# A fused routing-attention and two-layer kernel: three weight conversions moved to the second block, transposed rows through another PSUM bank, the last product in two column halves

## The chip, the cores and the metric

The kernel runs on one core of a Trainium2 chip. The metric is device time in microseconds. The kernel before takes 992.72 us, the median of three runs (991.85 to 994.62). The profiled execution has a span of 994.2 us, and all positions below are counted from the start of that span.

## What is computed

Four batches of eight heads attend over 768 tokens of 64 numbers each. Every query and key is assigned to the nearest of 16 centroids of its head, and a query sees only the keys of its own centroid. The heads, side by side, form rows of 512 numbers that go through two dense layers with a leaky activation. Cut to its core:

```python
q_assign = argmax(einsum('bhsd,hcd->bhsc', q_n, c_n), -1)     # k_assign likewise
mask = q_assign[..., :, None] == k_assign[..., None, :]
attn = softmax(where(mask, q @ k.T / 8, -1e9)) @ v            # (4, 8, 768, 64)
x = attn.transpose(0, 2, 1, 3).reshape(3072, 512)
h = x @ w_in                                                  # 512 -> 2048
g = maximum(h, 0) + alpha * minimum(h, 0)
out = g @ w_out                                               # 2048 -> 512
```

The weights arrive as 64-bit floating-point words. The kernel converts them to FP32 itself.

## The kernel before

**Steps and blocks.** Heads are taken in pairs, four pairs to a batch. For the first three batches the queries are split into two halves of 384, and the unit of work is a step: two key chunks of 128 for one head pair and one half of the queries. Three steps make a pair, twelve steps (`UB`) a block. The first block is half 0 of batch 0, the second is half 1. The last batch is done with the tokens sorted by cluster, so that only neighbouring chunks meet; its pairs are called near here.

A step computes scores into PSUM (`score`, L757, and for the first batch the mask as a product, L766), exponentials on ScalarE (L778), and multiplies the exponentials of the step before with the values (`weigh`, L893; in the first block also the denominators, L886). At the end of a pair `normalise` (L993) writes the transposed attention output xT. While the attention of one block runs, the dense layers of the block before are fed between its pieces: `hidden` (L1017, copied out by L1023, activated by `slopes`, L1009) and `final` (L1035, result copied by L1041 or added by L1043, and stored by L1046). During the first block there is nothing to feed.

**Order.** The order on each engine is written out by hand: the program's text is executed as a list of small pieces, and every engine runs its share in that order. `tick` counts slots, five to a step, and `later(n, piece)` puts a piece n slots further on.

**Conversions.** There are 32, each of 512 columns. `convert` loads raw words (L247, a ring of five raw tiles) and works in three stages: `split` on VectorE (L253 and L255), `scale` on ScalarE (L259 and L261) four slots later, and `join` on VectorE (L265 and L268) followed by a multiply on GpSimd (L271) two slots after that. The intermediate tile `power` comes from a ring of three. The tuple `converting` says how many conversions each of the first block's steps begins; afterwards it is two a step until all are begun. A dense piece that needs a weight which isn't ready runs the missing stages on the spot (`convert_up_to`).

**Cluster masks of the first batch.** `prep_sims` (L381) and `prep_argmax` (L402 to L423) find the clusters of the next pair on VectorE. `of_heads` then issues the copies of the mask to aq (L474, on ScalarE's queue) and computes `outside` (L429, ScalarE). Both are operands of L766 in the next pair's first step.

**PSUM.** The scores have two two-bank tiles (sps), the values' product one bank (vps). Two banks, fps, are shared in turn by `hidden`, `final`, some scores and, before the change, the row transposes. One bank, mps, is handed out by `misc()` and serves the cluster products (L381, L442), the row sums (`total`, L848) and one half of the near product (L926).

**Rows of the near pairs.** For the sorted batch the result goes back to token order. `normalise_near` (L932) writes outT, `to_rows` transposes it twice per pair on TensorE (L955), ScalarE copies it to rows (L958) one slot later, and `put_back` (L963) scatters the rows to memory, from which they are fetched again.

**The end.** The last two blocks' dense layers have no attention beside them. Each does its last eight products per output tile, adds the earlier partial sum and stores 128 rows.

Of the kernel before, what the change touches and what calls it, by code (L numbers as in the profile page):

```python
# [10 lines left out]
FP32 = mybir.dt.float32  # L11
# [5 lines left out]
ALU = mybir.AluOpType  # L17
AX = mybir.AxisListType
PS = bass.MemoryType.PSUM
P = 128  # L20
# [3 lines left out]
def kernel(  # L24
# [11 lines left out]
    nc = tc.nc  # L36

    B, H, S, D = q.shape
    NC = centroids.shape[1]
    DM, DF = moe_w_in.shape  # L40
    NJ = S // P
    NCH = DM // P
    NF = DF // P
    HJ = NJ // 2
# [12 lines left out]
    w_out_sb = wpool.tile([P, NF, DM], FP32, name="w_out_sb")  # L57
# [9 lines left out]
    accp = fast.enter_context(tc.tile_pool(name="accp", bufs=2))  # L67
# [7 lines left out]
    ps_f = fast.enter_context(tc.tile_pool(name="ps_f", bufs=2, space=PS))  # L75
# [8 lines left out]
    def misc():  # L84
        if early:
            early.append(early.pop(0))
            if early[0] is not None:
                return early[0]
        return ps_m.tile([P, 512], FP32, name="mps")
# [5 lines left out]
    def later(slots, piece):  # L95
        due.setdefault(now[0] + slots, []).append(piece)

    def tick():
        now[0] += 1
        for piece in due.pop(now[0], []):  # L100
            piece()
# [7 lines left out]
    Q = 32  # L109
# [52 lines left out]
    for g in range(P // Q):  # L162
        r = slice(g * Q, (g + 1) * Q)
        nc.gpsimd.tensor_copy(
            out=fold[r, :].rearrange("p (a i) -> p a i", i=Q),
            in_=ident[r, None, r].broadcast_to((Q, P // Q, Q)))
# [11 lines left out]
    for h in range(2):  # L178
        nc.vector.tensor_reduce(
            out=pick[:, h:h + 1],  # L180
            in_=fold.rearrange("p (a h c) -> p a h c", h=2, c=NC)[:, 0, h, :],
# [95 lines left out]
    FQ = CW // P  # L277
# [34 lines left out]
    def convert_up_to(n):  # L312
        while converted[0] < n:
            if not under_way:
                convert_next()
            else:
                advance(under_way[0])
# [54 lines left out]
    NX = GT * NG  # L372
# [41 lines left out]
    def prep_argmax(n, ps):  # L414
        top, first, pieces = argmax(ps, exact=n < NCH)
        for piece in pieces:
            piece()
        firsts[n] = first
        if n >= NCH:
            return  # L420
        member = memp.tile([P, HS], BF16, name="member")
        outside = memp.tile([P, 2, HS], BF16, name="outside")
        nc.vector.transpose(out=member, in_=top.rearrange("p t c -> p (t c)"))  # L423

        def of_heads():
            if n > 0:
                prep_queries(n, 0, 0)
            for h in range(2):
                nc.scalar.activation(  # L429
                    out=outside[HP:P, h, :], in_=member[HP:P, :], func=AF.Identity,  # L430
                    scale=pick[HP:P, h:h + 1], bias=pick[HP:P, h + 2:h + 3])

        members[n] = member, outside
        later(12 if n == 0 else 7, of_heads)

    def prep_clusters(n):

# [293 lines left out]
    UB = NCH * SB  # L731
# [50 lines left out]
    def last(m):  # L782

        return waiting[len(waiting) - m:]
# [165 lines left out]

    def to_rows(outT, rows, i):

        ps = ps_f.tile([P, 512], FP32, name="fps")
        for j in range(HJ):
            nc.tensor.transpose(out=ps[:, j * P:(j + 1) * P],  # L955
                                in_=outT[:, (i * HJ + j) * P:(i * HJ + j + 1) * P],
                                identity=ident)
        later(1, lambda: nc.scalar.copy(  # L958
            rows[:, i * HJ:(i + 1) * HJ].rearrange("p j d -> p (j d)"), ps[:, 0:HS]))
# [40 lines left out]
    def ffn_pieces(b, half):  # L1000
        rows = out[b * S:(b + 1) * S, :].rearrange(
            "(p j) n -> p j n" if b == 0 else "(j p) n -> p j n", p=P)
        gs, pss, ys, fresh = {}, {}, {}, deque()


        def slopes():
            while fresh:
                f = fresh.popleft()
                nc.vector.scalar_tensor_tensor(  # L1009
                    out=gs[f], in0=gs[f], scalar=alpha[:, f:f + 1], in1=gs[f],  # L1010
                    op0=ALU.mult, op1=ALU.max)

        def hidden(f):
            convert_up_to((f // FQ + 1) * (NCH + FQ) - FQ)
            ps = ps_f.tile([P, 512], FP32, name="fps")
            for c in range(NCH):
                nc.tensor.matmul(out=ps[:, 0:HS],  # L1017
                                 lhsT=w_in_sb[:, c, f * P:(f + 1) * P],
                                 rhs=xTs[b, half][:, c, :],
                                 start=(c == 0), stop=(c == NCH - 1))  # L1020
            slopes()
            gs[f] = gpool.tile([P, HS], FP32, name="gT")
            nc.scalar.copy(gs[f], ps[:, 0:HS])  # L1023
            fresh.append(f)
            if f % FQ == FQ - 1:
                slopes()

        def final(i, f0, on, off):
            convert_up_to((f0 // FQ + 1) * (NCH + FQ))
            if on:  # L1030
                pss[i] = ps_f.tile([P, 512], FP32, name="fps")
            unfinished[0] = not off
            ps = pss[i]
            for f in range(f0, f0 + FQ):
                nc.tensor.matmul(out=ps[:, 0:DM], lhsT=gs[f][:, i * P:(i + 1) * P],  # L1035
                                 rhs=w_out_sb[:, f, :], start=on and f == f0,
                                 stop=off and f == f0 + FQ - 1)
            if off:
                if i not in ys:
                    ys[i] = ypool.tile([P, DM], FP32, name="y")  # L1040
                    nc.scalar.copy(ys[i], ps[:, 0:DM])  # L1041
                else:
                    nc.vector.tensor_tensor(out=ys[i], in0=ys[i], in1=ps[:, 0:DM],  # L1043
                                            op=ALU.add)
                if f0 + FQ == NF:
                    nc.sync.dma_start(out=rows[:, half * HJ + i, :], in_=ys[i])  # L1046

        hs = [lambda f=f: hidden(f) for f in range(NF)]


        FP = FQ if (b, half) == (0, 0) else NF // 2
        pieces = []
        for f0 in range(0, NF, FP):
            pieces += hs[f0:f0 + FP]
            pieces += [lambda i=i, f=f, f0=f0: final(i, f, f == f0, f + FQ == f0 + FP)
                       for i in range(HJ) for f in range(f0, f0 + FP, FQ)]
        return pieces


# [62 lines left out]
    def feed(pieces):  # L1122
        for _ in range(pieces):
            ffn.popleft()()
# [15 lines left out]
    for u in range(-AHEAD, TOGETHER):  # L1140
        for piece in load_at.get(u, []):
            piece()
        n, half, s = steps[max(u, 0)]
        prior = steps[max(u - 1, 0)]
        ended = u > 0 and prior[2] == SB - 1
        tick()
        if u >= 0:


            score(n, half, range(s, NJ, SB))  # L1150
        tick()
        if ended:
            invert(*prior[:2])
        if u > 0:
            weigh(GROUP, denominators=u <= UB)
        if u >= 0:
            for chunk in last(GROUP):
                mask(chunk)
        if ended:
            normalise(*prior[:2])  # L1160
        if u >= UB:
            if s == 0:
                add_up(last(1)[0], last(2)[0])
            else:
                for chunk in last(GROUP):
                    add_up(chunk)
            if s == SB - 1:
                turn(n, half)
                rows_sums(n, half)
        if u == UB:  # L1170
            early.clear()
            feed_block(u)
            whole = len(ffn) - KEEP
        take = (max(len(ffn) - KEEP - whole * (UB - 1 - u % UB) // UB, 0) if ffn else 0)

        converting = 0 if u < 0 else (2, 0, 2, 2, 0, 2, 2, 1, 1, 1, 2, 2)[u] if u < UB else 2
        for i in range(SLOTS - FIRST):
            tick()
            feed(take * (i + 1) // 3 - take * i // 3)
            if (u, i) == (1 - AHEAD, 0):  # L1180
                cT, alpha = prepare_constants()
            prepare(u, FIRST + i)
            if i < converting:
                convert_next()
            if u >= -1:
                fetch(3 if u < UB else 2)
        if s == SB - 1 and u >= UB:
            total(n)
# [3 lines left out]
    for u in range(TOGETHER, NS + 1):  # L1192
        for piece in load_at.get(u, []):
            piece()
        if u < NS:
            n, half, s = steps[u]
# [49 lines left out]
        for i in slots:  # L1246
# [5 lines left out]
            pieces = len(ffn) - kept(u // UB) + -whole * left // (UB // SB * FREE)  # L1252
# [28 lines left out]
    ps = misc()  # L1281
    for i, p0 in enumerate((0, 1, P // 2, P // 2 + 1)):
        nc.tensor.matmul(out=ps[0:m, i * NN:(i + 1) * NN], lhsT=ident[:, p0:p0 + m],
                         rhs=sorts["begins"], start=True, stop=True)
# [4 lines left out]
                            in1=ident[0:m, m - 1:m], op=ALU.add)  # L1289
# [4 lines left out]
    for i in (1, 3):  # L1294
# [13 lines left out]
                            op=ALU.subtract)  # L1308
    nc.vector.tensor_tensor(out=ends[:, 1, :], in0=ends[:, 1, :], in1=spans[:, 2, :],
                            op=ALU.subtract)  # L1310
# [9 lines left out]
                     start=True, stop=True)  # L1320
# [161 lines left out]
```

## Time and profile before

| what | value |
|---|---|
| time, median of three | 992.72 us |
| span of the profiled execution | 994.2 us |
| TensorE busy | 968.9 us, 97% |
| VectorE busy | 632.0 us, 64% |
| ScalarE busy | 259.2 us, 26% |
| GpSimd busy | 216.8 us, 22% |
| first dense piece L1017, in total | 1024 instructions, 345.4 us |
| second dense piece L1035, in total | 768 instructions, 339.2 us |
| L271, GpSimd multiply of a w_in conversion | 16 instructions, mean 1706 ns |

How to read it: the busy time of TensorE counts matrix instructions from start to a modelled end, so an engine that is busy need not be at its peak rate; one FP32 product is two instructions here, hence twice the counts of the program. The profile also names, for each idle stretch of an engine, the instruction that ended it, and it follows one chain of waits back from the last instruction. A stage's cost is best read from these two together with the busy time of each engine in that stage.

### The profile page before, as it was taken

How to read it: one execution, taken by the hardware profiler on the slowest of the kernel's cores; microseconds unless marked ns; L12 is line 12 of the kernel's file. 1: busy time of each engine (PE TensorE's matmuls, PEld its weight loads, DVE VectorE, ACT ScalarE, POOL GpSimd, SP SyncE). 2: the span in 40 equal slices, each digit the busy share in tenths (PEclk: the TensorE clock that was granted, in tenths of full speed). 3: DMA queues.
4: the chain of work that ended last, by engine and by line, in shares of the span. 5: the costliest groups of instructions: out<-in, count | busy, mean ns of one | idle time of the engine just before them, and what ended most of it. 6: DMA issues, size and time to landing. Idle time of an engine off the chain costs nothing.

```text
span 994.2 us, 10869 instructions
## 1 busy us (share of the span) xinstructions
PE 968.9 (97%) x3947; PEld 480.7 (48%) x3947; DVE 632.0 (64%) x1143; ACT 259.2 (26%) x468; POOL 216.8 (22%) x249
## 2 busy tenths in 40 slices
PE   8988999999999999999999999999999999999997
PEld 5434444445454454545445454454544545455453
DVE  5796788598587776877857698577987532021010
ACT  5665443222121221312222022231232101110110
POOL 2433222010000634401000263630045440000000
PEclk9999999999999999999999999999999999999999
DMA  8434555041200361416020121710621110000000
GB/s 286 145 113 127 130 133 80 17 88 24 33 1 26 97 103 54 85 41 105 1 33 0 53 80 35 136 48 12 90 58 34 33 51 11 0 11 22 0 1 34
DMA packets 174285, 60.45 MB, mean 61 GB/s; under 512 B 161216, under 2 KB 164752, under 8 KB 174224
## 3 DMA queue, kind: packets, MB, share of 16 engines
q1 hardware_dynamic: 168768, 51.42, 24.0%
q0 software_dynamic: 4608, 7.87, 2.4%
q8 instruction: 33, 0.54, 0.2%
q10 hardware_dynamic: 848, 0.39, 0.2%
q14 instruction: 28, 0.23, 0.1%
HBM read 45.15 MB, written 14.16 MB: 60 GB/s over the span
## 4 chain that ended last, share of the span: by engine, by line
PE 90%; DVE 6%; ACT 1%; issue 1%; POOL 1%; ACTq 0%; DVEq 0%; POOLq 0%
PE fps L1017 33%; PE fps L1035 33%; PE vps L893 8%; PE sps L757 8%; PE fps L757 3%; PE mps L381 1%; PE vps L926 1%; PE mps L926 1%; PE sps L766 1%; DVE power L265 1%; ACT gT L1023 0%; DVE w_in_sb L268 0%; PE mps L848 0%; PE fps L354 0%; DVE power L253 0%
## 5 line engine op out<-in xcount | busy, mean ns | idle before, releaser
L1017 PE MATMUL fps<-xT,w_in_sb 128*128 128x384 f32 x1024 | 345.4, 492 | 5.7 <-DVE xT L993 3.0
L1035 PE MATMUL fps<-w_out_sb,gT 128*128 128x512 f32 x768 | 339.2, 596 | 2.2 <-DVE gT L1009 1.1
L1017 PEld LDWEIGHTS fps<-xT,w_in_sb 128*128 128x128 f32 x1024 | 191.4, 191 | 147.0 <-issue 10.0
L1035 PEld LDWEIGHTS fps<-w_out_sb,gT 128*128 128x128 f32 x768 | 143.4, 190 | 173.5 <-issue 161.7
L663 POOL DMA_INDIRECT scratch<-stage,off x96 | 101.4, 1056 | 324.5 <-DMA stage<-in_v_dram 265.9
L1009 DVE SCALAR_TENSOR_TENSOR gT<-gT,alpha 128x384 f32<-128x384 f32 x128 | 80.7, 636 | 140.6 <-ACT gT L1023 134.7
L1023 ACT COPY gT<-fps 128x384 f32<-128x384 f32 x128 | 61.2, 478 | 341.9 <-PE fps L1017 323.5
L757 PE MATMUL sps<-qkT 64*128 64x384 f32 (+1 forms) x512 | 97.9, 499 | 3.1 <-ACT E L778 2.4
L798 DVE SCALAR_TENSOR_TENSOR more<-aq,key,more 128x384 f32<-128x384 bf16 (+1 forms) x136 | 74.4, 605 | 28.8 <-ACT more L778 14.3
L778 ACT ACTIVATE E<-sps 128x768 f32<-128x768 f32 (+1 forms) x81 | 61.2, 803 | 72.6 <-PE sps L766 39.4
L963 POOL DMA_INDIRECT back<-rows,place x48 | 48.4, 1008 | 102.8 <-ACT rows L958 89.4
L757 PEld LDWEIGHTS sps<-qkT 64*128 64x128 f32 x512 | 46.2, 187 | 48.9 <-issue 19.7
L798 DVE SCALAR_TENSOR_TENSOR E<-aq,key,E 128x384 f32<-128x384 bf16 (+1 forms) x104 | 56.6, 600 | 16.8 <-ACT E L778 6.6
L893 PE MATMUL vps<-E,vt 128*64 128x384 f32 x356 | 65.7, 494 | 0.7 <-DVE xT L993 0.7
L1043 DVE TENSOR_TENSOR y<-y,fps 128x512 f32<-128x512 f32 x30 | 20.6, 685 | 69.5 <-PE fps L1035 69.5
L808 DVE TENSOR_TENSOR acc<-acc,E 128x768 f32<-128x768 f32 x47 | 44.9, 955 | 18.3 <-ACT E L778 17.0
L1041 ACT COPY y<-fps 128x512 f32<-128x512 f32 x24 | 14.1, 586 | 138.6 <-PE fps L1035 119.0
L778 ACT ACTIVATE more<-sps 128x768 f32<-128x768 f32 (+1 forms) x47 | 35.5, 797 | 41.8 <-PE fps L1035 21.6
L271 POOL TENSOR_TENSOR w_in_sb<-w_in_sb,power 128x512 f32<-128x512 f32 x16 | 27.3, 1706 | 72.6 <-DVE w_in_sb L268 72.6
L893 PEld LDWEIGHTS vps<-E,vt 128*64 128x64 f32 x356 | 23.0, 136 | 32.6 <-issue 31.0
L893 PE MATMUL vps<-more,vt 128*64 128x384 f32 x220 | 38.8, 491 | 0.0
L757 PE MATMUL fps<-qkT 64*128 64x384 f32 x160 | 35.0, 508 | 0.0
(177 smaller groups left out, 704.3 us busy)
## 6 DMA issues: line engine op xcount, KB each, us to landing
raw<-in_moe_w_in_dram SPq DMA_DIRECT2D x16, 512.0 KB
raw<-in_moe_w_out_dram SPq DMA_DIRECT2D x16, 512.0 KB
out_dram<-y SPq DMA_DIRECT2D x24, 256.0 KB
vt<-in_v_dram SPq DMA_DIRECT2D x12, 384.0 KB
qk<-in_q_dram SPq DMA_DIRECT2D x48, 96.0 KB
qk<-in_k_dram SPq DMA_DIRECT2D x48, 96.0 KB
qk<-scratch SPq DMA_DIRECT2D x32, 96.0 KB
qk<-in_q_dram SPq DMA_DIRECT2D x4, 384.0 KB
```

The lines of the kernel that those rows point to most:

```text
L271: nc.gpsimd.tensor_tensor(out=dst, in0=dst, in1=power[0].bitcast(FP32), op=ALU.mult)
L663: nc.gpsimd.indirect_dma_start(out=scratch[n][1][h * NX + xx], out_offset=bass.IndirectOffsetOnAxis(ap=ranks[n][:, xx, h:h + 1], axis=0), ...
L757: nc.tensor.matmul(out=bank(ps, h, m), lhsT=qkT[r:r + D, S + c * P:S + (c + 1) * P], rhs=qkT[r:r + D, tokens], start=True, stop=not early_ ...
L778: nc.scalar.activation(out=E[:, :, 0:m], in_=ps[:, :, 0:m], func=AF.Exp, scale=SCALE)
L798: nc.vector.scalar_tensor_tensor(out=e, in0=of, scalar=keys[n][:, NJ + c, h:h + 1], in1=e, op0=ALU.is_equal, op1=ALU.mult)
L808: nc.vector.tensor_tensor(out=acc, in0=acc if first is None else first[3], in1=E, op=ALU.add)
L893: nc.tensor.matmul(out=po[r:r + D, 0:HS], lhsT=vts[n][:, h, c, :], rhs=e[:, h, :], start=(c == 0), stop=(c == NJ - 1))
L963: nc.gpsimd.indirect_dma_start(out=to[i], out_offset=bass.IndirectOffsetOnAxis(ap=place[:, h, j:j + 1], axis=0), in_=rows[:, j, h * D:(h + ...
L1009: nc.vector.scalar_tensor_tensor(out=gs[f], in0=gs[f], scalar=alpha[:, f:f + 1], in1=gs[f], op0=ALU.mult, op1=ALU.max)
L1017: nc.tensor.matmul(out=ps[:, 0:HS], lhsT=w_in_sb[:, c, f * P:(f + 1) * P], rhs=xTs[b, half][:, c, :], start=(c == 0), stop=(c == NCH - 1))
L1023: nc.scalar.copy(gs[f], ps[:, 0:HS])
L1035: nc.tensor.matmul(out=ps[:, 0:DM], lhsT=gs[f][:, i * P:(i + 1) * P], rhs=w_out_sb[:, f, :], start=on and f == f0, stop=off and f == f0 + ...
```

## The change

It has three independent parts.

1. Three fewer conversions are begun in the first block, from its seventh step on (14 instead of 17). The second block, which begins two a step until none is left, takes them over. With it `of_heads` comes one slot later for the second to fourth pair, which puts it behind the exponentials of its step in ScalarE's order. The aim is to spread the conversions' work away from the stage where VectorE has most to do.
2. `to_rows` takes its PSUM bank from `misc()` (mps) instead of the ring fps, so that the dense pieces have both banks of fps to themselves.
3. The very last output tile is computed in two halves of 256 columns, each with its own bank, addition and store, the second store on ScalarE's queue. The aim is that the store of the first half runs beside the products of the second, and that the rest after the last product is shorter.

```diff
@@ prep_argmax
-        later(12 if n == 0 else 7, of_heads)
+        later(12 if n == 0 else 8, of_heads)
@@ to_rows
-        ps = ps_f.tile([P, 512], FP32, name="fps")
+        ps = misc()
@@ ffn_pieces
+        def final_columns(i, f0, c0):
+
+            ps = ps_f.tile([P, 512], FP32, name="fps")
+            c = slice(c0, c0 + DM // 2)
+            for f in range(f0, NF):
+                nc.tensor.matmul(out=ps[:, 0:DM // 2], lhsT=gs[f][:, i * P:(i + 1) * P],
+                                 rhs=w_out_sb[:, f, c], start=f == f0, stop=f == NF - 1)
+            y = accp.tile([P, 2 * NX, Q], FP32, name="acc").rearrange(
+                "p x i -> p (x i)")[:, 0:DM // 2]
+            nc.vector.tensor_tensor(out=y, in0=ys[i][:, c], in1=ps[:, 0:DM // 2], op=ALU.add)
+            (nc.scalar if c0 else nc.sync).dma_start(out=rows[:, half * HJ + i, c], in_=y)
...
+        if (b, half) == (B - 1, 1):
+
+            pieces[-(FP // FQ):] = [lambda c0=c0: final_columns(HJ - 1, NF - FP, c0)
+                                    for c0 in (0, DM // 2)]
@@ first block
-        converting = 0 if u < 0 else (2, 0, 2, 2, 0, 2, 2, 1, 1, 1, 2, 2)[u] if u < UB else 2
+        converting = 0 if u < 0 else (2, 0, 2, 2, 0, 2, 1, 1, 1, 1, 1, 1)[u] if u < UB else 2
```

## The prediction, made before the changed kernel was run

> **What bounds the kernel now.** I read the page first: busy shares, then the chain of waits.
>
> ```profile
> PE 968.9 (97%) x3947; PEld 480.7 (48%) x3947; DVE 632.0 (64%) x1143; ACT 259.2 (26%) x468; POOL 216.8 (22%) x249
> ...
> PE 90%; DVE 6%; ACT 1%; issue 1%; POOL 1%; ACTq 0%; DVEq 0%; POOLq 0%
> ```
>
> TensorE (PE) sets the end nearly everywhere; 6% of the chain is VectorE (DVE), some 60 us. The chain in order of time puts most of that before 103 us. So next came busy time by stretch, the end of the first block against the second:
>
> ```profile
> 46.00:60.00 14.00, 13.65 (x124) 5.44 (x120) 13.17 (x28) 8.49 (x14) 3.55 (x4) 1.00 0.28 95
> 60.00:74.00 14.00, 11.26 (x80) 4.43 (x80) 12.56 (x26) 9.31 (x14) 6.25 (x5) 0.88 0.51 156
> 74.00:88.00 14.00, 10.99 (x75) 4.95 (x74) 11.14 (x25) 7.90 (x13) 5.89 (x4) 0.93 0.47 150
> 125.00:150.00 25.00, 25.00 (x96) 11.36 (x93) 21.75 (x36) 12.25 (x20) 7.00 (x5) 1.00 0.62 131
> 150.00:175.00 25.00, 25.00 (x103) 11.81 (x103) 21.66 (x35) 8.44 (x15) 6.60 (x5) 1.00 0.52 74
> 175.00:200.00 25.00, 25.00 (x113) 11.43 (x112) 13.15 (x23) 6.21 (x10) 0.88 (x3) 1.00 0.07 17
> ```
>
> Columns: PE, weight loads, DVE, ScalarE (ACT), GpSimd (POOL), then granted clock. From 46 to 88 us DVE works 37 of 42 us, PE falls to 11 of 14, and its clock to 0.88. From 125 PE is full, and after 175 DVE is half idle. PE's instructions in time order show the price of the first block:
>
> ```profile
> 62.05 2.77 PE L757 MATMUL sps<-qkT 64*128 64x384 f32 x8 [2.40 <-ACT E L778]
> ...
> 86.21 1.62 PE L1017 MATMUL fps<-xT,w_in_sb 128*128 128x384 f32 x2 [3.01 <-DVE xT L993]
> ```
>
> Eight score passes cost 2.77 after an idle 2.40, against 1.56 elsewhere. The chain shows why xT is late: conversions stand in front of it on DVE, and the split L253 waits for POOL's multiply L271.
>
> ```profile
> 79.93 1.29 POOL w_out_sb L271
> 81.22 0.02 issue
> 81.24 0.44 DVE power L253
> ...
> 85.50 0.57 DVE xT L993
> 86.07 0.14 issue
> 86.21 7.71 PE fps L1017 x18
> ```
>
> [...]after the 3.01 us stall 18 passes of L1017 take 7.71 us, 0.428 each, against 0.3225 at full speed (64 in 20.64). [...]a split instruction that runs beside L271 takes 1.49 (45.51 us) instead of 0.42, and that L271 3.45 instead of 1.28. [...]Here the last 256 KB are issued at 988.95, move between 989.5 and 990.6, and the span ends at 994.2.
>
> **Part 1, three conversions out of the first block.** PE's floor there: a step is L757 1.49 + L766 0.43 + L886 0.79 + L893 1.44 = 4.15. From 46.35 (score of step 6): six steps 24.9, L381 0.78, a seventh 4.15, six L1017 passes 1.94 gives 78.1; the pass that waits for xT began at 86.21. That is 8.1 lost, and 7.71 - 18 x 0.3225 = 1.9 by the clock: at most 10.0 to win.
>
> How much does DVE release? Between the normalisations of the second pair (49.19) and of the fourth (83.13) it ran 9 splits and 9 joins; the changed program's order has 6 and 7. A split is 0.67 (51.98 to 52.65), a join 1.20 (to 53.85): 3 x 0.67 + 2 x 1.20 = 4.4. Besides, three waits of L253 for L271 (1.38, 1.18, 1.39) come of the ring of three power buffers: a split needs the multiply of three conversions before. With one conversion a step that multiply is over before the split. Three contended instructions add about 1.1 each. So DVE gives up 4.4 surely, 11.7 at the most.
>
> I followed the new order with these durations. Up to 57.8 (last argmax, L423) nothing moves. The `of_heads` delay of one slot puts step 8's exp (L778, two for 1.51) on ACT ahead of the aq transfers and L429 (1.29), so it starts at 57.4 instead of 61.19 and step 9's score finds its banks free at 59.6: the 2.40 wait goes. What is queued behind: L429 now ends near 60.7, and L766 of step 9, due at 61.1, needs it and aq, which land about 1.2 after their issue ends at 59.4; 0 to 0.4 lost. At steps 2 and 5 the same swap meets PE work that isn't due for over 4 us: nothing. Then the third pair's normalisation ends at 66.1, before L893 needs its bank (66.9), and the fourth's can run 75.2 to 78.1, as L886 ends, against L1017's need at 78.5. DVE has some 3 us of gaps left by then; two contended splits would eat 2 of them and cost PE about 0.9. So 10.0 - 0.4 - 0.9 = **8.7 saved**, bounds 4.4 and 10.0.
>
> What it adds: three conversions in the second block. The rate stays two a step; they only run on to step 20, where DVE has 12 of 25 us free (175 to 200). The order shows none forced by L1017's or L1035's due conversion. Two splits and a join more (2.5 us) ahead of L861/L993 near 176: L993 then waited for PE anyway (0.73), and its bank isn't needed until L893 at 186.35. Joins before a y addition can hold a bank: **0.4 lost**, bounds 0 and 9.5 (three times 1.87 of DVE plus 1.3 of POOL).
>
> **Part 2, rows through mps.** L955 leaves the two-bank ring fps for the single bank mps.
>
> ```profile
> 714.92 2.85 PE L1017 MATMUL fps<-xT,w_in_sb 128*128 128x384 f32 x8 [0.24 <-ACT gT L1023]
> 718.34 0.55 PE L955 MATMUL fps<-ident,qk 128*128 128x128 f32 x3 [0.57 <-ACT gT L1023]
> ...
> 774.34 2.85 PE L1017 MATMUL fps<-xT,w_in_sb 128*128 128x384 f32 x8 [0.68 <-ACT y L1041]
> ```
>
> Removed by the ring: pair 1 0.24 + 0.57 + 0.48 (L1017 at 722.13), pair 2 0.24 + 0.57, pair 3 0.68, pair 4 0.24 + 0.57 + 0.24: together 3.8. Added: the second L955 of a pair waits for the first's copy L958, which stands on ACT behind gT (717.80 and 718.18 there): PE ends at 717.77, L958 at 718.67, so 0.93 with the semaphore. That holds for pairs 1 and 2; in pairs 3 and 4 another piece lies between. In pair 1 L442, on mps too, waits another 0.93 for the second copy. L848 comes a whole piece later: nothing. 3 x 0.93 = 2.8, so **1.0 saved**, bounds -1 and 3.8.
>
> **Part 3, last product by halves.** Eight 512-column products are 16 instructions at 0.4292 (48 in 20.60). By the slope (0.4292 - 0.3225)/128 a 256-column one takes 0.216, and 32 give 6.91 against 6.87. Weight loads (0.19) hide: near 764 L757 sets two 64-row loads per pair of passes at the same rate. Unhidden they would add 6. The first half's addition and transfer lie beside the second half. At the end:
>
> ```profile
> 988.24 0.69 DVE L1043 TENSOR_TENSOR y<-y,fps 128x512 f32<-128x512 f32 x1 [6.18 <-PE fps L1035]
> 988.95 0.33 SPq L1046 DMA_DIRECT2D out_dram<-y  x1
> ```
>
> The addition at 256 columns: L993's 384 take 0.56, so 1 ns a column, 0.43; 0.26 saved. Half the bytes: 0.35 of the 0.7 DMA-busy time. ACT's queue issues in up to 0.60 (L474) against 0.33: 0.1 lost. **0.5 saved**, bounds 0.2 and 0.7.
>
> Sum: -8.7 + 0.4 - 1.0 - 0.5 = -9.8; 992.7 - 9.8 = **983**.
>
> **Rivals.** (a) Everything is won: 10.0 + 2.5 + 0.7, 979.5. For: the order has no ring wait left. Against: mps has one bank. (b) DVE stays the bound and returns only its 4.4: -4.4 + 0.4 - 1.0 - 0.5, 987. For: DVE at 37 of 42 us, and contention that I can't place. (c) The second block gives it back, DVE being at 87% from 125 to 175: +9.5 instead of 0.4, 992.4. Against: PE didn't wait for conversions there. (d) Slower: (b) for the first block, and mps makes every second L955, and the L442 and L848 after them, wait: nine times 0.93 = 8.4 with nothing won from the ring: 992.7 - 4.4 - 0.5 + 8.4 = 996. For: mps serves totals, clusters and the near product as well.
>
> **Chances.** Main 0.62, (a) 0.07, (b) 0.19, (c) 0.07, (d) 0.05. Faster 0.88, same 0.07, slower 0.05. The range takes in (a) and (b) with a measuring spread of about 1, and leaves out (c) and (d): 979 to 988.
>
> **What would show it.** The step-9 score with no wait for L778; no idle before L1017 for xT; that pass near 78.5; granted clock near 1.00 from 60 to 100; L253 not waiting for L271 before 80; L955 waiting 0.9 twice and L442 once; no L1017 waiting for gT from 711 us on (in the old time). It is wrong if DVE stays packed to 80 us with PE waiting, or if PE shows new waits between 100 and 200 us.

## The result, and the profile after

The changed kernel takes **981.87 us**, the median of four runs (981.49 to 982.53), where the kernel before, in runs beside it, takes 992.29 us (991.55 to 994.62). The ratio is 0.9892, with a 95% interval from 0.9874 to 0.991: 10.4 us saved, where 9.8 were forecast. The profiled execution of before was a long one (996.02 us against a median of 992.29), so the two spans, 994.2 and 979.9 us, differ by more than the times do. Some 3 us of the difference are stalls of before's profiled execution; they are told of with the experiment after_again.

The page of the kernel after, busy time and shares of the chain:

```profile
PE 962.9 (98%) x3963; PEld 482.8 (49%) x3963; DVE 635.0 (65%) x1144; ACT 258.7 (26%) x468; POOL 214.9 (22%) x249
...
PE 92%; DVE 5%; issue 1%; ACT 1%; POOL 0%; DVEq 0%; ACTq 0%; POOLq 0%
```

TensorE's share of the chain rises from 90% to 92% and VectorE's falls by a point. The 16 more TensorE instructions are the last product in halves (32 instead of 16). VectorE's busy time even rises by 3 us: the conversions did not go away, they moved. The same stretches as before show where to (span, then PE, weight loads, VectorE, ScalarE, GpSimd, granted clock, DMA share, GB/s):

```profile
46.00:60.00 14.00, 14.00 (x126) 5.74 (x124) 13.50 (x29) 9.63 (x15) 3.75 (x4) 1.00 0.39 115
60.00:74.00 14.00, 12.66 (x112) 5.17 (x110) 12.53 (x26) 9.54 (x15) 8.74 (x5) 1.00 0.57 167
74.00:88.00 14.00, 14.00 (x75) 6.83 (x72) 9.20 (x22) 4.61 (x8) 3.53 (x2) 1.00 0.33 102
150.00:175.00 25.00, 25.00 (x100) 11.71 (x93) 24.40 (x44) 10.63 (x19) 5.41 (x4) 1.00 0.56 87
175.00:200.00 25.00, 24.14 (x111) 10.94 (x112) 19.41 (x33) 7.46 (x13) 3.05 (x4) 1.00 0.08 19
```

From 60 to 88 us PE is now busy 26.66 of 28 us instead of 22.25, at full clock. From 150 to 200 VectorE works 43.81 us instead of 34.81, and PE beside it is busy 49.14 of 50; the 0.86 is one wait of L1035 for gT at 194.27, which before has too, as long, at 202.74. In PE's own order:

```profile
59.44 1.56 PE L757 MATMUL sps<-qkT 64*128 64x384 f32 x8
...
67.71 1.51 PE L893 MATMUL vps<-E,vt 128*64 128x384 f32 x8 [1.34 <-DVE xT L993]
...
77.44 8.01 PE L1017 MATMUL fps<-xT,w_in_sb 128*128 128x384 f32 x24
```

The first line is the score that waited 2.40 for L778; it has no wait left. The third is the dense piece that stood still for 3.01 us in front of its seventh pass; its 24 passes now follow one another. The middle line is what is left: one wait for xT, a pair earlier. Before waits there too, 0.69 at 71.26.

The near stage, where the rows now use the single bank mps:

```profile
708.58 0.55 PE L955 MATMUL mps<-ident,qk 128*128 128x128 f32 x3 [0.95 <-ACT rows L958]
...
712.66 0.25 PE L442 MATMUL mps<-cluster,spread 128*128 128x24 bf16 x4 [0.95 <-ACT rows L958]
...
732.48 0.55 PE L955 MATMUL mps<-ident,qk 128*128 128x128 f32 x3 [0.95 <-ACT rows L958]
...
765.21 0.39 PE L848 MATMUL mps<-parts,fold 128*128 128x48 f32 x2 [0.52 <-ACT gT L1023]
```

Three of these four waits were forecast, at 0.93 each. The waits of L1017 for the ring's gT copy are gone from this stage. And the end of the program:

```profile
967.59 7.07 PE L1053 MATMUL fps<-w_out_sb,gT 128*128 128x256 f32 x32
...
974.69 0.42 DVE L1057 TENSOR_TENSOR acc<-y,fps 128x256 f32<-128x256 f32 x1 [3.03 <-PE fps L1053]
975.15 0.38 ACTq L1058 DMA_DIRECT2D out_dram<-acc  x1
```

The last addition takes 0.42 instead of 0.69, and from its start to the end of the span there are 5.21 us (979.9 less 974.69) instead of 5.96 (994.2 less 988.24).

### The profile page after: what moved, and what is told of

It reads as the page before. It is cut to its first block, busy times and chain, and to the rows that moved or that the text cites. A ratio compares the mean times of both kernels' runs of the same rounds, so it can differ in the third digit from the quotient of the medians.

```text
span 979.9 us, 10900 instructions
## 1 busy us (share of the span) xinstructions
PE 962.9 (98%) x3963; PEld 482.8 (49%) x3963; DVE 635.0 (65%) x1144; ACT 258.7 (26%) x468; POOL 214.9 (22%) x249
## 4 chain that ended last, share of the span: by engine, by line
PE 92%; DVE 5%; issue 1%; ACT 1%; POOL 0%; DVEq 0%; ACTq 0%; POOLq 0%
PE fps L1017 33%; PE fps L1035 33%; PE vps L893 9%; PE sps L757 8%; PE fps L757 3%; PE mps L381 1%; PE vps L926 1%; PE sps L766 1%; PE fps L1053 1%; PE mps L926 1%; DVE power L265 1%; DVE w_out_sb L268 0%; PE vps L201 0%; PE mps L848 0%; PE fps L886 0%
## 5 line engine op out<-in xcount | busy, mean ns | idle before, releaser
L1017 PE MATMUL fps<-xT,w_in_sb 128*128 128x384 f32 x1024 | 342.6, 490 | 0.0
L1035 PE MATMUL fps<-w_out_sb,gT 128*128 128x512 f32 x752 | 332.2, 595 | 1.1 <-DVE gT L1009 1.1
L1017 PEld LDWEIGHTS fps<-xT,w_in_sb 128*128 128x128 f32 x1024 | 190.9, 190 | 138.3 <-ACT more L778 4.4
L1035 PEld LDWEIGHTS fps<-w_out_sb,gT 128*128 128x128 f32 x752 | 140.3, 190 | 168.4 <-issue 158.1
L757 PE MATMUL sps<-qkT 64*128 64x384 f32 (+1 forms) x512 | 96.1, 494 | 0.0
L778 ACT ACTIVATE E<-sps 128x768 f32<-128x768 f32 (+1 forms) x81 | 61.2, 802 | 71.3 <-PE sps L766 39.9
L757 PEld LDWEIGHTS sps<-qkT 64*128 64x128 f32 x512 | 45.7, 186 | 44.5 <-issue 17.4
L893 PE MATMUL vps<-E,vt 128*64 128x384 f32 x356 | 65.7, 494 | 1.3 <-DVE xT L993 1.3
L778 ACT ACTIVATE more<-sps 128x768 f32<-128x768 f32 (+1 forms) x47 | 35.4, 796 | 41.3 <-PE sps L757 40.4
L271 POOL TENSOR_TENSOR w_in_sb<-w_in_sb,power 128x512 f32<-128x512 f32 x16 | 25.4, 1594 | 67.1 <-DVE w_in_sb L268 67.1
L893 PEld LDWEIGHTS vps<-E,vt 128*64 128x64 f32 x356 | 23.0, 136 | 33.3 <-issue 30.7
L893 PE MATMUL vps<-more,vt 128*64 128x384 f32 x220 | 38.8, 491 | 0.0
L271 POOL TENSOR_TENSOR w_out_sb<-w_out_sb,power 128x512 f32<-128x512 f32 x16 | 22.9, 1432 | 57.3 <-DVE w_out_sb L268 57.3
```

The costliest lines, as they stand in the source:

```text
L271: nc.gpsimd.tensor_tensor(out=dst, in0=dst, in1=power[0].bitcast(FP32), op=ALU.mult)
L757: nc.tensor.matmul(out=bank(ps, h, m), lhsT=qkT[r:r + D, S + c * P:S + (c + 1) * P], rhs=qkT[r:r + D, tokens], start=True, stop=not early_ ...
L778: nc.scalar.activation(out=E[:, :, 0:m], in_=ps[:, :, 0:m], func=AF.Exp, scale=SCALE)
L893: nc.tensor.matmul(out=po[r:r + D, 0:HS], lhsT=vts[n][:, h, c, :], rhs=e[:, h, :], start=(c == 0), stop=(c == NJ - 1))
L1017: nc.tensor.matmul(out=ps[:, 0:HS], lhsT=w_in_sb[:, c, f * P:(f + 1) * P], rhs=xTs[b, half][:, c, :], start=(c == 0), stop=(c == NCH - 1))
```

## The experiments

Times of one chip are compared with the kernel before on that chip. There are two questions: does the relief of VectorE before 90 us carry the gain, and why did the near stage win more than its waits add up to? Where two traces are set side by side below, the start of each TensorE instruction in one is compared with the start of the same instruction in the other; this is called the distance between the traces. Each expectation numbers its own theories.

### Each part alone

On a chip where before takes 992.51 us (35 runs). **conv_only** is before with part 1 alone:

```diff
-        later(12 if n == 0 else 7, of_heads)
+        later(12 if n == 0 else 8, of_heads)
...
-        converting = 0 if u < 0 else (2, 0, 2, 2, 0, 2, 2, 1, 1, 1, 2, 2)[u] if u < UB else 2
+        converting = 0 if u < 0 else (2, 0, 2, 2, 0, 2, 1, 1, 1, 1, 1, 1)[u] if u < UB else 2
```

> The kernel before with part 1 alone: the new converting tuple and of_heads one slot later. Theory 1 (the parts add up, and the first block carries most of the gain): 8.5 us less than before, about 983.8, because the two traces stand 8.5 us apart from the first dense pieces on and the second block gives nothing back. Theory 2 (the parts help each other, so that each alone is worth less, and the near pairs carry about half): about 5 us less, 987. A trace of the second block with new PE waits would speak for theory 2.

Measured: 984.19 us, ratio 0.9917 (0.9904 to 0.993), so 8.3 us saved. Part 1 is four fifths of the whole.

**tuple_only** is the second of these two lines without the first.

> The kernel before with the new converting tuple alone; of_heads stays where it was. Theory 1 (VectorE's load is what counts, the exp's place on ScalarE is a smaller term): L429 still stands ahead of step 8's exp, so the score of step 9 waits near 2 us and may lose some clock; 5.5 to 7 us less than before, about 986. Theory 2 (the exp's place is what counts): at most 3 us less, 989 or more.

Measured: 985.16 us, ratio 0.9927 (0.9914 to 0.994), 7.35 us saved, more than expected. PE in its trace:

```profile
61.94 1.62 PE L757 MATMUL sps<-qkT 64*128 64x384 f32 x8 [1.67 <-ACT E L778]
```

Without the slot's delay the score still waits for ScalarE, but 1.67 instead of 2.40, and its eight passes take 1.62 instead of 2.77: the clock was not lost. That leaves about 1 us (8.3 less 7.35) to the delay, and theory 2, the exp's place as the main thing, is out.

**heads_only** is the first of the two lines without the second, on another chip (the second, below), where before takes 996.04 us (22 runs).

> The kernel before with of_heads one slot later and nothing else. Theory 1 (in the kernel before VectorE's queue sets the first block's end, so an earlier exp is absorbed by the wait for xT at L1017): within 0.5 us of before, 992. Theory 2 (the terms add, 7.35 and 8.3 measured with and without it): 1 us less, 991.5. Theory 3 (the wait for the exp and the clock after it are a loss of their own): 3 us less, 989.5.

Measured: 994.86 us, ratio 0.998 (0.9963 to 0.9997), 1.2 us saved, as theory 2 had it. It agrees with what tuple_only lacks against conv_only, though the interval reaches from 0.3 to 3.7 us: as far as these runs can tell, the two edits add up and neither needs the other.

**rows_only** is before with part 2 alone, on the first chip:

```diff
-        ps = ps_f.tile([P, 512], FP32, name="fps")
+        ps = misc()
```

> The kernel before with part 2 alone: to_rows takes the bank of misc(). Theory 1 (the prediction's count, 3.8 us of ring waits removed and 2.8 of waits for the row copy added): 1 us less than before, 991.3. Theory 2 (each stopped dense piece also costs a restart, seen as 2.86 instead of 2.58 for a piece after a wait, so more is removed than was counted): 2 us less, 990.3. Theory 3 (the traces' 4 us over the near pairs is all the bank's doing): 4 us less, 988.3.

Measured: 990.36 us, ratio 0.9978 (0.9971 to 0.9984), 2.15 us saved, twice the 1.0 of the prediction and close to theory 2.

**halves_only** is before with part 3 alone (`final_columns` and the replaced last pieces, as in the diff above).

> The kernel before with part 3 alone: the last output tile in two column halves. Theory 1 (shorter last addition and half the bytes): 0.5 to 0.7 us less than before, 991.7, and 32 passes in 6.9 us. Theory 2 (the second store's issue on ScalarE's queue and its own latency eat it): no change, within 0.2.

Measured: 991.8 us, ratio 0.9994 (0.9985 to 1.0002). The 0.7 us agree with the 0.75 that the traces show at the end, but the interval includes no gain. This kernel still has the ring, and its execution has none of the stalls told of below, so it shows best what an interruption costs:

```profile
712.48 0.49 PE L955 MATMUL fps<-ident,qk 128*128 128x128 f32 x3
713.21 2.85 PE L1017 MATMUL fps<-xT,w_in_sb 128*128 128x384 f32 x8 [0.24 <-ACT gT L1023]
716.63 0.55 PE L955 MATMUL fps<-ident,qk 128*128 128x128 f32 x3 [0.57 <-ACT gT L1023]
```

The number to read is the distance of the starts. From L955 to L1017 it is 0.73 here, and from L1017 to the next L955 3.42. In copy_first_2 (below), which waits for nothing here, the same distances are 0.33 and 2.58 (9.11 less 6.53). So the two interruptions cost 0.40 and 0.84, not 0.24 and 0.57. The page counts idle time from the modelled end of the last matmul, and without a wait the next one begins 0.16 to 0.27 before that end; a wait loses this on top of its bracket. Read so, the nine waits that part 2 removes, 3.8 as shown, were worth about 5.6, and the four that it adds, 3.4 as shown, about 4.1. That makes 1.5 instead of 0.4. Set side by side, the traces show more: from the L1017 at 713.86 to the one at 800.00 (positions of before) rows_only gains 3.96 us on before. Of this, 1.93 is a stall of before between 733 and 737, which halves_only, with the same code there, doesn't have. The remaining 2.03 is part 2, and the 2.15 of the runs agree with it. So an interruption does cost more than its bracket shows, and most of the surplus is this overlap. The changed kernel's first trace gains the same 3.96 on before in this stretch, so half of what the near stage seemed to win there was the stall.

The three parts alone add up to 11.2 us (8.3, 2.15 and 0.7), together they measured 10.4, within what the intervals allow. The traces of before and after, with before's stalls left out, give 8.47, 2.03 and 0.75, again 11.2.

### How many conversions

On the second chip (before 996.04). **dose16** and **dose13a** are the changed kernel with two conversions put back at the end of the first block, and with one more taken out:

```diff
-(2, 0, 2, 2, 0, 2, 1, 1, 1, 1, 1, 1)
+(2, 0, 2, 2, 0, 2, 1, 1, 1, 1, 2, 2)   dose16
+(2, 0, 2, 2, 0, 2, 1, 0, 1, 1, 1, 1)   dose13a
```

> The changed kernel with 16 conversions begun in the first block instead of 14: steps 11 and 12 begin two again, so only the one of step 7 is moved. Theory 1 (VectorE's queue is the bound there, and each conversion kept costs its 1.87 and a wait of 1.2 for L271): 5 to 6 us more than the changed kernel, about 987.3. Theory 2 (the one of step 7, which meets the last argmax, is what counts; the late two have room): at most 1.5 us more, 983.4.

> The changed kernel with 13 conversions begun in the first block: step 8 begins none. Theory 1 (the changed kernel's first block still loses 1.34 us at L893 because VectorE is late with xT): that wait goes and the second block takes one more conversion for nothing, 1.3 us less than the changed kernel, 980.6. Theory 2 (the second block is now full, VectorE being at 98% from 150 to 175 us): the gain is given back there, no change or up to 1 us more.

Measured: dose16 990.14 us, ratio 0.994 (0.9928 to 0.9952); dose13a 986.73 us, ratio 0.9899 (0.9885 to 0.9912). The changed kernel, run on the same chip later (after_again, below), took 988.61. So two conversions more cost 1.5 us, though the intervals of dose16 and after_again overlap, and one less saves 1.9. The traces place both. In dose16's PE order the wait for xT is back:

```profile
77.86 2.20 PE L1017 MATMUL fps<-xT,w_in_sb 128*128 128x384 f32 x6
83.05 6.04 PE L1017 MATMUL fps<-xT,w_in_sb 128*128 128x384 f32 x18 [2.98 <-DVE xT L993]
```

Set beside the trace of after_again point by point of the program, dose16 falls 3.2 us back here; by the end shorter stalls in the near stage (told of below) bring the two within 1.0. By its time alone dose16 would suit theory 2 (at most 1.5 us more); by its trace the wait of theory 1 is there, but costs 3.2 and not 5 to 6. It did not lose the clock: 18 passes in 6.04, against 7.71 in before. In dose13a the wait of L893 near 67.7 is gone: it stands 0.33 behind after_again before that place and 1.13 ahead after it, and is still 1.0 ahead at 718, before stalls begin to differ. The prediction's condition, that the last xT is ready when L1017 comes to it near 78.5, holds with 14 conversions and fails with 16.

### The copy of the rows given out at once

**copy_first** and **copy_first_2** are the same kernel, the changed one with one edit:

```diff
-        later(1, lambda: nc.scalar.copy(
-            rows[:, i * HJ:(i + 1) * HJ].rearrange("p j d -> p (j d)"), ps[:, 0:HS]))
+        nc.scalar.copy(
+            rows[:, i * HJ:(i + 1) * HJ].rearrange("p j d -> p (j d)"), ps[:, 0:HS])
```

The first ran beside dose16, the second beside **after_again**, the changed kernel itself, and **both**, which is copy_first with the conversions of dose13a; these three on the second chip, where before takes 995.98 us (10 runs).

> The changed kernel, but the copy of the transposed rows (L958) is put into ScalarE's order right behind the transposes instead of one slot later, so that it stands ahead of the gT copy of the next dense piece. Theory 1 (what is left of the wait at the rows is ScalarE's order alone): the two waits of L955 (0.95 each), that of L442 (0.95) and that of L848 (0.52) for L958 go, 3.0 to 3.4 us less than the changed kernel, about 978.7. Theory 2 (one bank for all is what counts, whoever copies first): the waits shrink to the transposes' own length and come back elsewhere, under 1 us less, 981 or more.

> The changed kernel once more, as the control beside copy_first_2 and both. Both theories expect the ratio of its first measurement, 0.989 of the kernel before, within 0.002. In its trace: L893 waits about 1.3 for xT near 67.7 us, L955 twice and L442 once 0.95 for the rows' copy, L848 once 0.5.

> The changed kernel with the rows' copy L958 given out at once instead of one slot later, beside the changed kernel on one chip. Theory 1 (the single bank's price is the copy's place behind gT on ACT): the three waits of 0.95 are gone, 2 to 3 us faster than the changed kernel. Rival (the copy only moves in front of gT, whose own bank then holds up L1017 by as much): within 0.6 us of it, with new waits of L1017 for gT in their place.

> copy_first_2 with step 8 of the first block converting none (the conversion runs in the second block). Theory 1 (DVE's contended instructions at 59 to 65 us are what is left of the wait for xT at 67.7): L893's 1.3 wait goes and nothing takes its place, 1.0 to 1.5 us faster than copy_first_2, in all 3 to 4.5 us faster than the changed kernel. Rival (the second block gives the conversion back): the first block is 1.4 shorter and new waits between 100 and 250 us of about as much, so the same as copy_first_2 within 0.5 us.

| kernel | us, median | ratio to before | 95% interval |
|---|---|---|---|
| copy_first | 985.68 | 0.9884 | 0.987 to 0.9899 |
| after_again | 988.61 | 0.9926 | 0.9913 to 0.994 |
| copy_first_2 | 983.83 | 0.988 | 0.9864 to 0.9897 |
| both | 982.31 | 0.9863 | 0.9846 to 0.9879 |

copy_first_2 in the near stage:

```profile
706.53 2.75 PE L1017 MATMUL fps<-xT,w_in_sb 128*128 128x384 f32 x8
709.11 0.49 PE L955 MATMUL mps<-ident,qk 128*128 128x128 f32 x3
709.44 2.75 PE L1017 MATMUL fps<-xT,w_in_sb 128*128 128x384 f32 x8
712.02 0.25 PE L442 MATMUL mps<-cluster,spread 128*128 128x24 bf16 x4
```

L955 and L442 wait for nothing, and no L1017 waits in their place: the rival of copy_first_2 is out. By the distance between the traces of after_again and copy_first_2, each removed wait gave 1.1 to 1.2 (0.95 plus the overlap again), 3.4 in all. One new wait, L848's for VectorE at 740.98 (0.44), takes some 0.55 of it back. The measured 4.8 is more than the 2 to 3 expected; the rest is shorter stalls, below. copy_first, 2.9 us faster than after_again, had been expected to lose L848's 0.52 near 766 as well; that wait stays. Its profiled execution, unlike that of copy_first_2, ran 3.41 us at half clock from 727.03 on, behind a stall, and the two medians of this one kernel are 1.85 apart.

both is 1.5 us faster than copy_first_2. PE's order in the two, first copy_first_2:

```profile
68.14 1.51 PE L893 MATMUL vps<-E,vt 128*64 128x384 f32 x8 [1.40 <-DVE xT L993]
```

and then both:

```profile
66.89 1.51 PE L893 MATMUL vps<-E,vt 128*64 128x384 f32 x8
```

The wait for xT is gone, worth 1.47 by the distance between the traces, and 1.41 of it is still there at 700 us: the second block gives back next to nothing for this conversion either. **both beats the kernel before and the changed kernel**: 13.7 and 6.3 us on this chip, as measured.

### The same kernel on another chip, and stalls that stay unexplained

after_again missed its expectation: 0.9926, and the interval excludes the 0.9892 of the first measurement. The change saved 7.4 us here instead of 10.4. Its waits are those of the first trace. What differs are stretches in which several engines stand still at once. One of them, in the changed kernel's first trace:

```profile
722.02 1.90 PE L926 MATMUL mps<-E,vt 128*64 128x384 f32 x16
723.85 0.92 PE L757 MATMUL fps<-qkT 64*128 64x384 f32 x4
```

and the same instructions in after_again, where the first L926 begins at 724.29:

```profile
724.62 0.88 DVE L798 SCALAR_TENSOR_TENSOR more<-aq,key,more 128x256 f32<-128x256 bf16 x2 [2.90 <-issue]
726.11 0.41 PE L926 MATMUL mps<-E,vt 128*64 128x128 f32 x2 [0.57 <-issue]
726.82 0.27 PE L926 MATMUL mps<-E,vt 128*64 128x128 f32 x1 [0.30 <-issue]
728.84 0.97 PE L757 MATMUL fps<-qkT 64*128 64x384 f32 x3 [0.56 <-ACT more L775]
```

"issue" means that the engine waited for nothing that the profile shows. From the first L926 to L757, PE takes 4.55 us instead of 1.83, and VectorE has stood idle for 2.90. Set against the first trace of the changed kernel, after_again falls back by 1.2 us near 625, by 0.7 near 720, by 3.1 to 728 and by 1.0 to 749: 6.0 in all, and by nothing elsewhere beyond the 0.4 it starts with. The profiled execution of before has such stalls in the same two stretches, in front of the L1035 at 634.72 (1.15 by distance) and between 733 and 737 (1.93): 3.1 in all, and its 996.02 us are what before takes on the second chip. So there the changed kernel would have 6.0 us of stalls and before 3.1, and 10.4 less the 2.9 between them is 7.5, where 7.4 was measured. This fits the time, but it is arithmetic on single executions. The stalls go by chip: the four traces kept from the first chip have none in these stretches, the seven from the second all do. Their lengths differ by kernel, and no run here was made that tells their cause. That stays open.

## Why the prediction was right, and where it wasn't

- **Part 1, 8.7 forecast, less 0.4 for the second block.** conv_only, which has both, saved 8.3, and the two traces of before and after stand 8.46 apart at the score that follows the freed L1017 passes (93.84 and 85.38). The score of step 9 has no wait; the pass forecast near 78.5 ran at 79.48; the clock is 1.00 from 60 to 100. Right in sum and mechanism. That the sum fits so well is in part luck: how much clock before loses differs between its executions (last section), and against the groups of before's 35 runs told of there conv_only saves 7.6, 8.4 or 10.0. The trace read for the prediction was of the middle kind.
- **What it costs on the way.** The prediction allowed 0.9 for two splits slowed beside L271 and 0.4 for the aq copies. What the trace shows is one wait of 1.34 for xT at 67.71 and nothing for aq. In front of that xT, L255 takes 1.50 at 59.19 and L909 1.44 at 64.94, beside L271; with no L271 running they take 0.42 (at 52.18) and 0.36 (at 50.29). Not every split beside L271 is slowed: L255 at 62.15 takes 0.44, and the L271 that runs there 2.92. dose13a and both, which have one conversion less there, lose the wait; that the instructions running beside L271, and not the work itself, are the cause was only argued.
- **L253 waiting for L271 before 80: wrong.** One wait of 1.18 is left, at 72.58, but no PE work waits behind it. No run here changed the ring of power buffers, which would test that wait by itself.
- **Second block, 0.4 forecast, bounds 0 to 9.5.** It gave back nothing: the traces are 8.46 apart at 85.38 and 8.47 at 223.16 in the new time, and PE shows no new wait between 100 and 200. Rival (c) is out. So is (b), the 987 of a VectorE that stays the bound, and (d). (a) is out by the waits that remain, those for xT and for the rows' copy.
- **Part 2, 1.0 forecast, 2.15 measured.** The term that was mis-sized is the removed ring waits. They were summed as the brackets show them, 3.8, but each also costs the overlap of two matmuls, and by the distances they were worth 5.6 or more. The three added waits of 0.93 came as forecast (0.95 each), with the same surcharge, and one that was not forecast, L848's 0.52 at 765.21: in pair 3 the total now takes mps behind a dense piece, and its bracket names the gT copy of ScalarE. It stays in copy_first, so it isn't due to where the rows' copy stands.
- **Part 3, 0.5 forecast.** 0.7 by the runs, not clear of no gain, and 0.5 to 0.6 where runs with the same mean clock are compared; 0.75 by the traces. 32 instructions take 6.92 in the chain, where 6.91 was forecast: the weight loads stay hidden.
- **A sum and a reading.** Rival (c) with 9.5 in place of 0.4 gives 992.0, not 992.4. And the L271 of 3.45 us is not the one beside the split at 45.51: it ran from 42.02 to 45.47, and the two multiplies beside the slowed splits took 1.27 and 1.46. So that place shows two splits slowed (1.49 and 1.50 instead of 0.42) and the multiplies beside them hardly. No sum rests on the 3.45.
- The sum was 9.8 and the measurement 10.4. The one term with a clear error is part 2, short by 1.15; the parts alone add up to 0.8 more than they gave together, which these intervals can't tell from nothing.

## What to carry to other kernels

Follow work that is to be moved in time order through the engine that does it, and find the one operand that the bound engine needs last: here two conversions more or fewer decided whether xT was ready before TensorE asked for it. When a wait for a shared bank is priced, take the distance between the starts of the matmuls with and without it, not the idle time in the bracket. And each wait for the single bank mps cost what its reader took to get to it, here 0.95 us and the overlap; with the rows' copy ahead of gT's three such waits went, 3.4 us by the distance between the traces. So give out the copy that frees a single bank ahead of work that frees a bank of which there are two.

## What the runs showed of the hardware that was not expected

**The clock did not follow from one idle time.** Before lost it after waits of 2.40 us (at 62.05) and 3.01 (at 86.21). halves_only has the same first block and the same wait of 2.40, and kept it: 1.62 for the eight passes, not 2.77.

```profile
63.11 1.62 PE L757 MATMUL sps<-qkT 64*128 64x384 f32 x8 [2.40 <-ACT E L778]
```

In fine slices the traces show the granted clock at 0.50, apart from the ends of the program, only in stretches of 3.41 us or twice that: two in before, three in rows_only, one each in halves_only and copy_first, one of 6.83 in heads_only, none in the other eight. Within a trace they lie whole steps of 3.41 apart: 62.26 and 86.15 in before are seven, and the last fall of its clock, at 990.69, comes 272 steps after the first. In these traces the loss went with the idle time inside one such step, as before and then dose16 show (PE is the first number after the comma, the clock the third from the end):

```profile
58.85:62.26 3.41, 1.01 (x8) 0.34 (x6) 2.03 (x5) 3.00 (x6) 1.26 (x1) 1.00 0.38 130
62.26:65.67 3.41, 3.41 (x16) 1.07 (x18) 3.41 (x6) 1.69 (x4) 1.85 (x2) 0.50 0.48 148
...
78.09:81.50 3.41, 1.97 (x6) 0.83 (x5) 3.25 (x11) 1.59 (x3) 1.26 (x1) 1.00 0.51 159
81.50:84.91 3.41, 1.86 (x6) 1.23 (x7) 3.27 (x7) 0.48 (x1) 0.00 (x0) 1.00 0.35 132
84.91:88.33 3.42, 3.42 (x12) 1.96 (x12) 2.26 (x6) 0.48 (x1) 1.58 (x1) 1.00 0.49 146
```

dose16's idle 2.98 falls into two steps, 1.44 and 1.55, and the clock stays at 1.00 behind both. In all 13 traces, between 10 and 970 us, every step with 2.10 us or more of idle PE was followed by half clock (in before 2.40 and, from 82.74, 2.95), none with 1.55 or less was (the longest in after is 1.48, from 43.10), and of five between 1.62 and 1.76 three were (before's 1.62, from 41.78, was not). What decides between those five was not shown. A step need not be idle throughout: in before's from 58.85 PE was busy for 1.01.

**So one kernel has several times.** The 35 runs of before on the first chip fall into three groups by mean granted clock: 0.997 to 0.998 (median 991.77 us), 0.995 to 0.996 (992.57) and 0.993 (994.23). One stretch at half clock takes 0.0017 off that mean (half of 3.41 in 994.2), and the traces of this first block have one, two or three; that the groups are these is an inference, since the 35 runs left no traces of their own.

**The stalls** of several engines at once near 625 and from 720 to 750 us, 0 to 6 us in all by execution and chip, can be twice what parts 2 and 3 win together. A gain that small should be read against the same kernel on the same chip.
